# One tile pair's gate transposes on TensorE instead of by DMA, with re-planned engine orders, in a fused attention and MLP kernel

## The chip, the cores and the metric

One core of a Trainium2 chip. The metric is device time in microseconds (us) of one execution, lower is better. A profiled span is 1.7 to 1.9 us shorter than the time of the same execution in the runs of the kernel before, so spans are compared with spans and times with times. TensorE, VectorE, ScalarE, GpSimd and SyncE appear in the profile as PE (PEld for its weight loads), DVE, ACT, POOL and SP. The kernel before took 177.51 us (median of 3 runs, 177.42 to 177.81).

## The reference

Two branches work on one layer norm of x (2048 tokens, 448 columns, bf16) and are added up with x. Cut to what matters:

```python
xn = layernorm(x)
# A: linear attention, 16 heads of 28
q, k, v = split(xn @ wqkv)
phi_q = cat(softmax(q @ w_phi), softmax(-q @ w_phi))       # phi_k alike
o = (phi_q @ (phi_k.T @ v)) / (phi_q @ sum(phi_k) + 1e-6)
A = o @ wo
# B: token-shift mixer, then an MLP of 1792
h = gelu(layernorm(xn) @ w1)
hs = shift_tokens(h, (1, -1, 2, -2)) @ w2                  # four column groups, four shifts
x1 = xn + hs
B = x1 + gelu(layernorm(x1) @ w3) @ w4
return x + A + B
```

## The kernel before

The kernel is written for one core as a list of tasks. A planner places the tasks by a model (durations, PSUM slots, DMA delays) and by a table of ranks and earliest times; a recorder then emits each engine's instructions in that order and derives all semaphores. So most of a change of orders stands in a table of numbers, not in code. All instructions carry the line of a helper: L197 matmul, L201 transpose, L205 ScalarE, L209 VectorE and GpSimd, L212 DMA, L215 DMA transpose.

A second-layer tile pair (`W2`) gives the layer-normed gate tiles `g_tok`. They are transposed into `gT`, the right-hand side of the last stage's `H` matmuls (H = w3, then gelu; F = w4 and wo). In the kernel before every pair goes by a DMA transpose (`DMA_TRANSPOSE` in the profile), as do the transposes into `hT` that feed the second layer (indices shortened, cuts marked by dots):

```python
ga.append(P.add("ga%d" % i, dve, 320, ...))        # normalised gate tile into g_tok
def gd(t, j=j):
    R.dmaT(gT[:, slot, 2 * (j % 2):2 * (j % 2) + 2, :, :]..., g_tok[:, P.slot[("g", j)], :, :]...)
g_ready[i0] = g_ready[i1] = P.add("gD%d" % j, "SP", TI, G_RANK[j], ga, gd, gk, lag=TL2)
...
for d, i in enumerate((i0, i1)):                   # final addition and store, tile by tile
    def fin(t, ...):
        R.ew(dve, "tensor_tensor", outb[:, ob(i), u:v], bank(P.slot[k], d)[:, 0:v - u], xs[:, slot(i), u:v], op=ALU.add)
    def stor(t, ...):
        R.dma(outr[:, res_of(i), u:v], outb[:, ob(i), u:v], t.eng)
```

The softmax here doesn't subtract the row's maximum and nothing guards it: scores larger than these inputs give would overflow.

## Time and profile before

The prediction below shows the page, stretches, waits and chain of this kernel; they are not repeated. What matters of them:

| | kernel before |
|---|---|
| span, TensorE busy | 176.1 us, 169.2 us |
| waits of TensorE after the warm-up's start | wq 0.4, wv 0.5, hT 0.9, gT 0.3 us |
| H and F stage, 72.8 to 173.4 us | 0.11 us of idle |

TensorE is the bound, so the table is read from the waits: apart from the amount of TensorE's own work, only what ends one of them, or the start and the end around that work, can change the time.

The timeline of the kernel before from the last matmuls on (start, duration, engine, instruction, count, idle before):

```profile
172.91 1.45 SPq L212 DMA_DIRECT2D out_dram<-vaug  x2
173.31 0.69 DVE L209 TENSOR_TENSOR vaug<-ps,vaug 128x224 bf16<-128x224 f32 x2 [0.80 <-PE ps L197]
173.73 0.38 ACTq L212 DMA_DIRECT2D out_dram<-vaug  x1
```

Two additions of one half tile each, and a store behind each: the first goes out on the ACT queue at 173.73 while the second addition still runs. The SP entry at 172.91 merges two issues, one of them the last store, at 174.02.

### The profile page before, as it was taken

What the parts mean: (1) busy time and instruction counts of PE and PEld (TensorE: products, weight loads), DVE (VectorE), ACT (ScalarE), POOL (GpSimd) and SP (SyncE); (2) the same over time, 40 slices, a digit from 0 to 9 for tenths busy, and PEclk for the clock granted to TensorE, in tenths of its full rate; (3) what the DMA queues carried; (4) which work ended last, traced back from release to release, by engine and by line L of the source; (5) the groups of instructions that cost most, each with busy time, mean ns of one, the idle gap of its engine ahead of it and who ended that gap; (6) DMA issues with size and microseconds to landing.
All of it is one profiled execution on the core that took longest, in us unless ns stands there. A gap on an engine that the chain in (4) does not pass through costs nothing.

```text
span 176.1 us, 4846 instructions
## 1 busy us (share of the span) xinstructions
PE 169.2 (96%) x2080; PEld 111.4 (63%) x2080; DVE 116.4 (66%) x300; ACT 81.4 (46%) x116; POOL 77.8 (44%) x105
## 2 busy tenths in 40 slices
PE   5999999999999979999999999999999999999993
PEld 4766566676666665455555667655676666766793
DVE  3879999977995798995986655830654554370133
ACT  3398999999999510264557100327001561200000
POOL 7515578699339334035432253640037141261080
PEclk9999999999999999999999999999999999999999
DMA  6993444599918496625054616130010403313022
GB/s 146 279 339 83 72 83 91 101 360 327 331 49 162 77 122 123 119 32 93 0 98 86 120 27 149 53 63 0 0 56 26 89 0 63 60 52 63 0 86 78
DMA packets 41766, 18.30 MB, mean 104 GB/s; under 512 B 33552, under 2 KB 40848, under 8 KB 41744
## 3 DMA queue, kind: packets, MB, share of 16 engines
q1 hardware_dynamic: 41136, 17.91, 43.2%
q8 instruction: 16, 0.26, 0.6%
q10 hardware_dynamic: 608, 0.08, 0.3%
q14 instruction: 6, 0.05, 0.1%
HBM read 8.28 MB, written 1.84 MB: 57 GB/s over the span
## 4 chain that ended last, share of the span: by engine, by line
PE 86%; DMA 8%; SPq 3%; issue 1%; DVE 0%; DVEq 0%
PE ps L197 86%; DMA wv<-in_A_wqkv_dram 4%; SPq L212 3%; DMA hT<-hq 3%; DMA gT<-wv 2%; DVE vaug L209 0%; DVEq L169 0%; SPq L215 0%
## 5 line engine op out<-in xcount | busy, mean ns | idle before, releaser
L205 ACT ACTIVATE phik<-ps 128x1024 bf16<-128x1024 f32 (+1 forms) x44 | 41.3, 997 | 45.4 <-PE ps L197 45.4
L209 DVE TENSOR_TENSOR vaug<-ps,vaug 128x464 f32<-128x464 f32 (+3 forms) x66 | 32.8, 505 | 21.3 <-PE ps L197 15.9
L197 PE MATMUL ps<-w,phik 64*128 64x448 bf16 (+1 forms) x504 | 45.9, 328 | 0.0
L197 PE MATMUL ps<-gT,w 64*128 64x512 bf16 x392 | 44.5, 376 | 0.3 <-DMA gT<-wv 0.3
L197 PEld LDWEIGHTS ps<-w,phik 64*128 64x128 bf16 x504 | 29.5, 94 | 12.3 <-ACT phik L205 0.3
L197 PEld LDWEIGHTS ps<-gT,w 64*128 64x128 bf16 x392 | 23.0, 94 | 17.4 <-DVE vaug L209 0.7
L209 POOL TENSOR_TENSOR xnT<-vaug 128x224 bf16<-128x224 f32 x32 | 17.3, 564 | 27.7 <-DVE vaug L209 27.7
L209 POOL TENSOR_TENSOR vaug<-xn,xtok 128x448 f32<-128x448 bf16 x16 | 16.4, 1037 | 28.5 <-DVE vaug L209 26.4
L209 POOL TENSOR_TENSOR phik<-phik,ksum 128x896 bf16<-128x896 bf16 x14 | 24.1, 1749 | 8.2 <-DVE ksum L209 8.2
L209 POOL TENSOR_TENSOR rs<-rs,mhalf 128x2 f32<-128x2 f32 (+1 forms) x17 | 11.5, 683 | 28.3 <-DVE rs L209 22.0
L205 ACT ACTIVATE eq<-ps 120x1024 bf16<-120x1024 f32 (+1 forms) x18 | 17.5, 1045 | 6.1 <-PE ps L201 4.9
L209 DVE TENSOR_REDUCE ksum<-phik 128x32 f32<-128x896 bf16 x16 | 16.6, 1059 | 1.1 <-ACT phik L205 1.0
L209 DVE RECIPROCAL vaug<-ps 128x16 f32<-128x16 f32 x16 | 4.1, 254 | 19.1 <-PE ps L197 19.1
L197 PE MATMUL ps<-wo,xnT 64*128 64x448 bf16 (+1 forms) x126 | 14.1, 328 | 0.0
L197 PE MATMUL ps<-wv,xnT 64*128 64x448 bf16 x112 | 13.6, 349 | 0.5 <-DMA wv<-in_A_wqkv_dram 0.5
L197 PE MATMUL ps<-xnT,hq 64*120 64x512 bf16 x112 | 13.6, 377 | 0.0
L197 PE MATMUL ps<-wpk,xnT 64*128 64x448 bf16 x112 | 13.2, 349 | 0.0
L197 PE MATMUL ps<-w,hT 64*128 64x448 bf16 x56 | 12.1, 349 | 0.9 <-DMA hT<-hq 0.9
L197 PE MATMUL ps<-w2s,hT 64*128 64x448 bf16 x56 | 12.1, 350 | 0.0
L209 DVE BATCH_NORM_STATS2 st<-xtok 128x6 f32<-128x448 bf16 x16 | 9.2, 614 | 3.2 <-DMA xtok<-in_A_x_dram 3.2
L197 PE MATMUL ps<-w,xnT 64*128 64x448 bf16 x112 | 11.2, 349 | 0.0
L205 ACT ACTIVATE hq<-ps,fs 128x224 bf16<-128x224 f32 x32 | 11.0, 493 | 0.2
(71 smaller groups left out, 174.5 us busy)
## 6 DMA issues: line engine op xcount, KB each, us to landing
w<-in_B_w_dram SPq DMA_DIRECT2D x2, 896.0 KB, 7.0
w<-in_B_w_dram SPq DMA_DIRECT2D x1, 1568.0 KB, 12.3
out_dram<-vaug SPq DMA_DIRECT2D x14, 112.0 KB, 1.7
xtok<-in_A_x_dram SPq DMA_DIRECT2D x3, 448.0 KB, 7.0
eq<-in_A_wqkv_dram SPq DMA_DIRECT2D x2, 336.0 KB, 3.7
w<-in_B_w_dram SPq DMA_DIRECT2D x2, 336.0 KB, 7.3
wv<-in_A_wqkv_dram SPq DMA_DIRECT2D x1, 336.0 KB, 6.5
w2s<-in_B_w_dram SPq DMA_DIRECT2D x1, 336.0 KB, 5.4
```

Source lines behind the costliest of these rows:

```text
L197: self.op("PE", lambda e: e.matmul(out, lhsT, rhs, start=start, stop=stop, skip_group_check=True), [out], [lhsT, rhs], after=after)
L205: self.op("ACT", lambda e: e.activation(out, in_, func, **kw), [out], [in_] + aps)
L209: self.op(eng, lambda e: getattr(e, name)(out, *args, **kw), [out], aps)
L212: self.op(eng, lambda e: e.dma_start(out, in_), [out], [in_], dma=True)
```

## The change

Its intent is to take one of the DMA transposes out of the queue that TensorE waits for, and to plan all engine orders again with the delays of DMA transposes in the model. Four parts:

```diff
+        G_PE, G_ACT = (1,), ()
+            if j in G_PE:
+                def gtr(t, j=j, k2=k2):                       # gP1: eight TensorE transposes into PSUM
+                    for d in range(2):
+                        v = bank(P.slot[k2], d).bitcast(BF16)
+                        for c in range(4):
+                            R.tr(v[:, 128 * c:128 * c + 128], g_tok[:, slot, d, 128 * c:128 * c + 128], ident[:, :])
+                ...                                           # gPc2, gPc3: two copies PSUM -> gT (ACT or DVE)
+                continue                                      # no gD1
@@ planner's load model, and every rank and earliest time (two tables, left out)
-        RATE = {"x2": 5.4, "x4": 4.0, "x8": 2.6, "x12": 2.6}
+        RATE = {"x8": 3.0, "x12": 3.0, "w10": 3.0, "w11": 3.0, "w12": 3.0}
@@ zeros for the warm-up matmuls
+        z_spin = P.add("z_spin", dve, 350, -31, [], lambda t: R.ew(dve, "memset", kvq[:, 0:1, :, :], 0.0))
-            R.ew(dve, "memset", kvq[:, :, :, :], 0.0)
+            R.ew(dve, "memset", kvq[:, 1:2, :, :], 0.0)
@@ final additions and stores: one for a pair of tiles (18 stores become 9)
-                    for d, i in enumerate((i0, i1)):
-                            R.ew(dve, "tensor_tensor", outb[:, ob(i), u:v], bank(P.slot[k], d)[...], xs[...], op=ALU.add)
-                            R.dma(outr[:, res_of(i), u:v], outb[:, ob(i), u:v], t.eng)
+                        R.ew(dve, "tensor_tensor", rows(outb, "ob"), both(P.slot[k])[:, :, 0:v - u], rows(xs, "xs"), op=ALU.add)
+                        R.dma(outr[:, res_of(i0):res_of(i0) + 2, u:v], rows(outb, "ob"), t.eng)
```

The new orders in words: wv is loaded after w1; K0, K1, Q0, Q1 come before the first V; the two wrap-around matmuls (`nudge`) no longer stand together; TensorE runs one block of phik x vaug matmuls (`kv0`) before the fourth hT pair, where the kernel before runs two (`kv0`, `kv1`); one second-layer pair moves into the F stage.

## The prediction

> **What bounds the kernel now.** I read the busy times of the page first, then the table of stretches, the waits of TensorE, the chain that ended last, and the DMA issues.
>
> ```profile
> span 176.1 us, 4846 instructions
> PE 169.2 (96%) x2080; PEld 111.4 (63%) x2080; DVE 116.4 (66%) x300; ACT 81.4 (46%) x116; POOL 77.8 (44%) x105
> ```
>
> TensorE is busy for 169.2 of 176.1 us, so 6.9 us is all that any re-ordering could win. The stretches say where it lies (columns: busy time and instructions of each engine, then granted clock, DMA share, GB/s):
>
> ```profile
> 0.00:12.00 12.00, 9.69 (x110) 7.92 (x112) 7.17 (x29) 5.83 (x8) 6.39 (x23) 1.00 0.84 247
> 12.00:60.80 48.80, 48.23 (x491) 31.31 (x490) 42.87 (x92) 45.47 (x73) 32.35 (x26) 1.00 0.62 162
> 60.80:72.80 12.00, 10.76 (x208) 6.88 (x207) 11.23 (x25) 1.87 (x5) 3.41 (x4) 1.00 0.88 139
> 72.80:173.40 100.60, 100.49 (x1276) 65.32 (x1276) 54.49 (x156) 28.20 (x31) 35.62 (x52) 1.00 0.26 55
> 173.40:176.10 2.70, 0.00 (x0) 0.00 (x0) 0.60 (x2) 0.00 (x0) 0.00 (x0) 1.00 0.30 83
> ```
>
> The fourth stretch, 57% of the span, has 0.11 us of TensorE idle: nothing to win there, much to lose. The last 2.7 us are final additions, the last store's 1.6 us from issue to landing, and the end. What remains is named by the waits of TensorE (total, times, longest):
>
> ```profile
> PE ps L197 <- DVE kvq L209: 1.9, 1, 1.9
> PE ps L197 <- DMA hT<-hq: 0.9, 1, 0.9
> PE ps L197 <- DMA wv<-in_A_wqkv_dram: 0.5, 1, 0.5
> PE ps L201 <- DMA eq<-in_A_wqkv_dram: 0.4, 1, 0.4
> PE ps L197 <- DMA gT<-wv: 0.3, 1, 0.3
> ```
>
> [...]The other four sum to 2.1 us[...]. The chain shows both and what stood in front:
>
> ```profile
> 59.02 4.92 DMA hT<-hq
> 63.94 0.14 issue
> 64.08 5.09 PE ps L197 x92
> 69.17 0.05 SPq L215
> 69.22 0.04 issue
> 69.26 3.31 DMA gT<-wv
> 72.57 0.25 issue
> 72.82 100.50 PE ps L197 x1262
> ```
>
> At 63.94 the fourth transposed hidden tile pair lands, 4.92 us after its issue, and TensorE has waited for it. At 72.57 the gate tiles of pair 1 land; their issue had stood until 69.26 behind another transpose of the same queue, though the gate tiles were written by VectorE at about 66.9. This is the wait that the change aims at, and it costs 0.32 us.
>
> [...]
>
> ```profile
> 11.42 0.61 PE L201 MATMUL ps<-ident,xn 128*128 128x128 bf16 x8
> gT<-wv SPq DMA_TRANSPOSE x8, 3.3
> ```
>
> Eight on TensorE take 0.61 us in all, so they pipeline; a whole pair by DMA takes 3.3 us to land, its issue 1.24 us. [...]the 3.0 us minimum seen for these transposes [...]says that they must be issued early or hidden. [...]warm-up matmuls start every 0.20 us at first and every 0.10 us after about 6.4 us, 4.5 us from the first.
>
> **The change, part by part.**
>
> *Pair 1's transpose on TensorE.* Removes one of eight gT transposes from the queue (1.3 us of issue, 3.3 us of latency). Adds eight 128x128 transposes: 8 x 56 ns (spacing of the same instruction at 11.4 us) = 0.45 us of TensorE, which is the bound. They stand between two full-array kv groups, so they cost no extra change of array mode. Adds two evictions on ScalarE at about 0.5 us each (the same shape, xnT<-ps 128x512, took 0.59 us for one and 1.09 us for two); ScalarE is idle for 7.4 us in that stretch, so these are free. Gain: the 0.32 us wait. Net: +0.13 us.
>
> *The new orders.* In the compared orders, wv is loaded last of the early weights, and K0, K1, Q0, Q1 run before V0 and V1. So the 0.53 us wait for wv, which now lands at 13.29, goes: V starts some 4 x 1.4 = 5.6 us later. But ScalarE then has a fold eviction (0.86 us) and two xnT evictions (0.5 us each) to do before K1, and VectorE has tile 4's statistics (0.57 us) before the copy that tiles 2 and 3 need. From the durations of the trace I get K0 0.2 us later than its 11.96 us, and 0.25 us of waits at K1 and Q0. Net of the start: -0.1, plus 0.19 us of a stall at 29.1 that need not recur: -0.3 us.
>
> *The middle.* One V eviction moves from ScalarE to VectorE (2 instead of 3 there), worth 0.82 us, but the order of Q2, Q3 before K3 leaves ScalarE about 2 us without input near 25 us. So the 32 gelu evictions, now from 48.50 at 0.35 us each, begin at about 48.7. The fourth hT transpose then needs the 28th gelu and one wrapped block: 48.7 + 28 x 0.35 + 0.3 = 58.8, issue 59.0, against 59.02 now. With two more behind it in the queue it should land after 3.2 to 4.9 us, 62.2 to 63.9. TensorE reaches it at about 62.7 (first-layer matmuls to 56.7, three second-layer pairs 3 x 1.33, two nudges and one kv group 2.0). Wait left: about 0.6 of 0.93 us: -0.3 us. The nudges, now apart from kv, add two mode changes of about 0.08: +0.15 us.
>
> *Gate transposes by TensorE, in time.* VectorE finishes both gate tiles only after the addition of the fourth second-layer pair, at about 69.9; TensorE comes there at 70.3. No wait, but under half a microsecond of slack.
>
> *H stage.* The order puts the numerator groups and the first H blocks in other PSUM slots. The first numerator frees its slot after a queue of VectorE work, at about 82; a later H block wants that slot at about 81.2. I allow +0.3 us for this and its like, in a stretch that has no idle now.
>
> *Pairwise final addition and store.* One addition of 2x224 (about 0.6 us) for two of 0.38 us (0.69 us together), one store instead of two: the last landing 0.1 us earlier. Eighteen stores become nine; most were hidden.
>
> *Split memset.* Warm-up starts perhaps 0.6 us earlier[...]. 0.
>
> Sum: +0.13 - 0.3 - 0.3 + 0.15 + 0.3 - 0.1 = -0.1 us. The hand count sees only waits that I followed; a re-planned order[...] was probably made against just these waits and may remove more of the remaining 1.0 us than I found. I move my figure by -0.8 us for that, which is judgement and not working: about -0.9, that is 176.6 us.
>
> **Rivals.** (a) *All data waits go.* Take away 0.53 + 0.93 + 0.32 + 0.19 + part of the 0.4, add 0.6: -1.6 us, 175.9[...]. For it: a plan made for these very delays. Against: the hidden-tile wait hangs on ScalarE's gelu (93% busy in the second stretch), which the change hardly relieves. (b) *The wait only moves.* The first H block waits no more for gT by DMA but for ScalarE's copy, or the transposes wait for the gate tiles, since the fourth pair's addition now comes before them on VectorE (busy for 11.23 of 12 us there). Then 177.5 to 178.5. (c) *VectorE or PSUM slots become the bound in the H stage.* VectorE is 54% busy there on average, but single blocks have a few hundred ns of slack. One us of new stalls makes 178. (d) *DMA at the start:* x tiles before w1 and wv could bring statistics forward and the first K with them: up to -0.5 us.
>
> **Range and chances.** Two per cent is 3.55 us. To be faster by that, all four waits (2.1 us) would have to vanish, the added 0.6 us be free, and 1.5 us more come from the start or the end, where loads and the last store hold the time: 0.04. Slower by that needs 3.5 us of new stalls in orders that were planned with measured durations: 0.03. The range of 175.0 to 178.2 is (a) at its best to (b) and (c) together.
>
> **What would show it.** In the profile after: no wait on gT by DMA ahead of the first H block; eight ident,wv transposes of about 0.45 us between kv groups; no wait on wv; a wait on hT near 62 to 64 us, of 0 to 1 us; the first wpk matmul at 12.0 to 12.5; 100.5 us of H and F work (now with one second-layer pair in it) still nearly without idle; the last store 1.6 us from issue to landing. I am wrong if TensorE's idle after 12 us is above 3 us, or if the first K begins before 11.3 us, or if the hT wait is gone and the gelu ended before 58 us.

What no trace or run of this case shows, names of units among it, is cut out of it, and the cuts are marked. The sum: it came to -0.1 us, and -0.8 us of judgement made it about -0.9, that is 176.6 us. The 175 of rival (a) at its best, where the range begins, counted on a quicker start, and so did the reason why the split memset, put down as 0, might save time. "The other four" waits leave out the first, the 1.9 us before the warm-up matmuls; "both" are those for hT and gT.

Three of its statements are read from the matmul records of the kernel before. The transposes at 11.4 us start 56 ns apart and are recorded with 0.22 us each, so they overlap; those at 5.06 to 6.23 us still start 0.11 us apart. Pairs of 64-row matmuls start 0.19 us apart, and 0.28 us pass from such a pair to a 128-row matmul (60.59 to 60.87): 0.09 us for a change of array mode. In the changed kernel the eight transposes stand between 128-row matmuls, and starts there are 0.03 us (before the first) and 0.06 us (after the last) apart.

## The result, and the profile after

The changed kernel took 178.26 us (median of 6 runs, 178.05 to 178.52), the kernel before beside it 177.97 us (6 runs, 177.42 to 180.89, the slowest of them slow: over 1.5% above the fastest run of the same kernel; such runs here show a granted clock, the share of TensorE's full clock, of 0.981 wherever it is listed, as in b_kv2 and b_shift100). A ratio in this document is the mean time of one kernel's fast runs over that of the other's of the same rounds, so it is not quite the ratio of these medians: 1.0023, 95% interval 0.9999 to 1.0046. A second timing of the same kernel (a_same below) gave 1.0041 (1.0015 to 1.0068). So it is 0.2 to 0.4% slower (the first interval just includes no difference), within 2% as expected, but above the predicted range of 175.0 to 178.2, whose middle promised 0.9 us of gain.

The page of the changed kernel:

```profile
span 176.5 us, 4844 instructions
PE 169.4 (96%) x2088; PEld 105.2 (60%) x2088; DVE 113.3 (64%) x291; ACT 81.9 (46%) x118; POOL 79.6 (45%) x106
```

Eight more TensorE instructions (the transposes); on balance nine fewer on VectorE and two more on ScalarE. The same stretches as in the prediction, except that the last one runs to this kernel's end:

```profile
0.00:12.00 12.00, 9.42 (x110) 7.65 (x112) 7.79 (x32) 5.71 (x8) 6.38 (x23) 1.00 0.83 260
12.00:60.80 48.80, 48.74 (x493) 25.52 (x493) 40.81 (x93) 44.79 (x73) 34.19 (x27) 1.00 0.66 161
60.80:72.80 12.00, 10.77 (x201) 7.24 (x201) 10.63 (x24) 1.60 (x4) 4.11 (x5) 1.00 0.84 130
72.80:173.40 100.60, 100.48 (x1292) 64.81 (x1288) 53.49 (x146) 29.80 (x34) 34.88 (x51) 1.00 0.26 52
173.40:176.50 3.10, 0.00 (x0) 0.00 (x0) 0.54 (x1) 0.00 (x0) 0.00 (x0) 1.00 0.22 61
```

TensorE's idle grew from 2.31 to 2.58 us in the first stretch and fell from 0.57 to 0.06 in the second: the start gained 0.24 us, which the 0.2 us of added TensorE work takes. The third has the same 1.2 us of idle, the fourth is as full as before. The last is 0.4 us longer, and that is the difference of the two spans. The waits of TensorE:

```profile
PE ps L197 <- DVE kvq L209: 1.9, 1, 1.9
PE ps L197 <- DMA hT<-hq: 1.2, 1, 1.2
PE ps L201 <- DMA eq<-in_A_wqkv_dram: 0.7, 1, 0.7
```

Gone are the waits for wv and for gT. Grown is the wait for hT, from 0.9 to 1.2 us, and that for wq. The chain that ended last shows where hT stands and that the transposes took the place of gT:

```profile
58.22 4.79 DMA hT<-hq
63.01 0.14 issue
63.15 6.29 PE ps L197 x106
69.44 0.45 PE ps L201 x8
69.88 103.41 PE ps L197 x1318
173.32 0.62 DVE vaug L209
```

The fourth hT transpose is issued 0.8 us earlier than in the kernel before (58.22 against 59.02) and takes 4.79 us to land (4.92 there). TensorE is through with all that the order puts before it at 61.92, so it stands for 1.23 us. At 69.44 the eight transposes cost 0.45 us and wait for nothing.

The last matmul ends at about 173.3 in both kernels. What follows, in the timeline of the changed kernel:

```profile
173.32 0.62 DVE L209 TENSOR_TENSOR vaug<-ps,vaug 128x448 bf16<-128x448 f32 x1 [1.00 <-PE ps L197]
173.97 0.38 SPq L212 DMA_DIRECT2D out_dram<-vaug  x1
```

One addition of both half tiles, then one store of 112 KB. Read from the records of the trace (us):

```
                last matmul ends   last store: issue, landing, took   span ends   matmul to end
kernel before        173.30           174.02   175.61   1.59           176.11        2.81
changed kernel       173.28           173.97   175.78   1.81           176.53        3.25
```

The issue is 0.05 us earlier, but the larger store takes 0.22 us longer and lands 0.17 us later. Another 0.25 us come after the landing (0.75 us to the span's end instead of 0.50): in the changed kernel the last semaphore instruction of SP ends 0.3 us after those of the other engines, in the kernel before with them. The times show little of this last part: the two profiled executions took 178.05 and 177.84 us, 0.21 us apart, where their spans are 0.42 us apart.

### The profile page after: what moved, and what is told of

It is laid out like the page before. It is cut to its first block, busy times and chain, and to the rows that moved or that the text cites. A ratio compares the mean times of both kernels' runs of the same rounds, so it can differ in the third digit from the quotient of the medians.

```text
span 176.5 us, 4844 instructions
## 1 busy us (share of the span) xinstructions
PE 169.4 (96%) x2088; PEld 105.2 (60%) x2088; DVE 113.3 (64%) x291; ACT 81.9 (46%) x118; POOL 79.6 (45%) x106
## 4 chain that ended last, share of the span: by engine, by line
PE 91%; DMA 5%; SPq 2%; DVE 0%; issue 0%
PE ps L197 89%; DMA hT<-hq 3%; DMA eq<-in_A_wqkv_dram 2%; SPq L212 2%; PE ps L201 1%; DVE vaug L209 0%
## 5 line engine op out<-in xcount | busy, mean ns | idle before, releaser
L209 DVE TENSOR_TENSOR vaug<-ps,vaug 128x464 f32<-128x464 f32 (+3 forms) x57 | 31.8, 559 | 23.1 <-PE ps L197 17.4
L197 PE MATMUL ps<-gT,w 64*128 64x512 bf16 x392 | 45.1, 376 | 0.0
L197 PEld LDWEIGHTS ps<-gT,w 64*128 64x128 bf16 x392 | 21.5, 94 | 17.4 <-DVE vaug L209 0.2
L209 POOL TENSOR_TENSOR phik<-phik,ksum 128x896 bf16<-128x896 bf16 x15 | 25.8, 1757 | 4.3 <-DVE ksum L209 2.8
L197 PE MATMUL ps<-xnT,hq 64*120 64x512 bf16 x112 | 13.0, 377 | 0.0
L197 PE MATMUL ps<-wpk,xnT 64*128 64x448 bf16 x112 | 12.6, 349 | 0.1
L197 PE MATMUL ps<-wv,xnT 64*128 64x448 bf16 x112 | 12.3, 349 | 0.0
```

Source lines behind the costliest of these rows:

```text
L197: self.op("PE", lambda e: e.matmul(out, lhsT, rhs, start=start, stop=stop, skip_group_check=True), [out], [lhsT, rhs], after=after)
L209: self.op(eng, lambda e: getattr(e, name)(out, *args, **kw), [out], aps)
```

## The experiments

Fifteen variants ran, all correct. They also answer two questions of method. First, the landing of the wq load, on which the first folds wait, varies from 8.00 to 9.03 us between executions of kernels with the new load order and from 7.88 to 8.40 us in the four fast profiles with the old one, so two single profiles cannot be compared at their starts. I therefore take from each profile the time from that landing to the end of the last matmul ("wq to last matmul"). Second, that figure hardly scatters (165.42 and 165.50 us in two profiles with the order of before, 165.28, 165.18 and 165.09 in three with the new order), so it shows tenths of a microsecond where the times show only halves. (In the order of before, part of a late wq can hide behind the wait for wv, so its figure may also be a little lower.)

Runs share a chip and its runs of the kernel before: a_shift64, a_shift16, b_shift100 and a_tail one chip; a_same, a_kv1, a_gp_dma, b_gp, a_kv1_tail, a_wq, a_all and b_kv2 a second; b_pair, b_kv2_gp and a_kv12_tail a third. Medians are compared only within one chip.

Two theories of the hT wait were tested. **Fetch theory:** all over the trace a 16 KB packet appears on a DMA queue of kind "instruction", called a fetch here (16 of 16,384 bytes in each of the two kernels' profiles, 192 to 312 matmuls and weight loads apart, 250 on average, of 4,160 and 4,176), and takes 0.9 to 1.9 us; a DMA transpose on which one falls often lands 1 to 2 us late (the fourth hT of the changed kernel after 4.79 us, its first three after 3.05 to 3.21), and around it the packets of transposes nearly stop (in the changed kernel from some 200 in 0.25 us to 58, 10 and 44 from 62.0 us on, right after the fetch of 60.98 to 61.92). **Queue theory** (the prediction's): the transposes are late because three of them stand in the queue back to back.

The packet records of the changed kernel show what is late. All 1,024 data packets of the fourth hT had started before the fetch, and so had 30 of the 32 four-byte packets that close it; the last two came at 61.90 and 61.91, when the fetch ended. 15 of its 16 completions came at 61.27 to 61.43, the last at 63.01. The packets that stall from 62.0 on belong to the transpose behind it. Whether the fetch held one of the core's 16 DMA engines isn't shown: the records don't name a packet's engine. Where the fetch comes earlier, in a_shift16 below (60.06), the fourth hT's own data packets stall (from some 200 in 0.25 us to about 10, from 61.0 to 61.75).

### More TensorE instructions, to move the fetches: a_shift64, a_shift16, b_shift100

The columns of the warm-up matmuls are cut among more of them, which adds 64 (or 16, or 100) TensorE instructions before the first real work and changes nothing else:

```diff
-                R.mm(bank(P.slot[("ps", "spin")], 0)[:, 0:240], z[:, 0:128], z[:, 0:240], True, True)
+                m = 3 if n < 12 else 2
+                for j in range(m):
+                    R.mm(bank(P.slot[("ps", "spin")], 0)[:, 0:240 // m], z[:, 0:128], z[:, 0:240 // m], True, True)
```

> The changed kernel with 64 more TensorE instructions (32 more warm-up matmuls before the first real work; the columns of the warm-up are cut among them, so its length stays). Fetch theory: one of the 16 KB instruction-fetch packets moves from 60.98 us to about 58 us[...]; the 4th hT transpose (issued 58.22) then lands after about 3.1 us instead of 4.79, the wait of TensorE before the matmuls of that hT falls from 1.23 us of idle to under 0.3, and the time falls by 0.7 to 1.3 us, less up to 0.5 if another transpose (the one of hT 3, or xn tile 6, 7 or 15, over which a fetch would now fall) becomes late. Queue theory (the transposes land late because three of them stand back to back in the queue): landing 4.5 to 5 us, wait 1.1 to 1.3 us, time unchanged within 0.2 us.

Measured: 178.91 us, ratio 1.0071 (1.0050 to 1.0092), slower instead of faster. (In the changed kernel no DMA packet starts from 58.0 to 59.25 us, where the fetch was to go.) The waits:

```profile
PE ps L197 <- DVE kvq L209: 1.9, 1, 1.9
PE ps L197 <- DMA xnT<-xn: 1.0, 2, 0.8
PE ps L201 <- DMA eq<-in_A_wqkv_dram: 0.8, 1, 0.8
PE ps L197 <- DMA hT<-hq: 0.6, 1, 0.6
```

The hT wait halved, but a wait of 1.0 us for xn transposes is new. The fetches had moved, and the lateness with them: now the transposes of xn tiles 6, 7 and 15 (4.14, 3.56, 4.26 us instead of about 2.45) and of hT 3 (4.19 instead of 3.04) had a fetch on them, and those that had lost theirs (hT 7, gate pair 6) landed after 3.23 and 3.04 us instead of 3.91 and 4.71. Tile 15 is on the path. The fetch that I had wanted at 58 us came at 60.56, still on the fourth hT: it does not fall at an exact instruction (25 further on than in the changed kernel), and the late tile 15 had moved the rest. So the lateness went with the fetches again, and my forecast of the time failed.

> Control: the changed kernel with 16 more TensorE instructions (8 more warm-up matmuls). Fetch theory: the fetch moves only to about 60.2 us, still inside the packets of the 4th hT transpose, so its landing stays over 4 us and the time within 0.4 us of the changed kernel. Queue theory: no change either. What it tells apart from the run with 64 more is whether more and shorter warm-up matmuls by themselves change the time.

Measured: 177.78 us, ratio 1.0009 (0.9984 to 1.0034). Not the null result that I wrote: the fourth hT landed after 3.85 us, under the 4 us of the expectation, and its wait fell to

```profile
PE ps L197 <- DMA hT<-hq: 0.3, 1, 0.3
```

From wq to the last matmul it took 164.33 us, 0.85 less than a_same. No order was changed; three transposes still stand back to back. So queue position alone is not the cause; nor are the first three hT transposes of the changed kernel late (issued at 51.93, 53.62 and 54.97, landed after 3.06, 3.21 and 3.05 us), which stand as close to each other as the next three. And a hole in this place costs about what it seems to cost: 0.85 us for a wait that is 0.8 us shorter (0.3 against 1.1).

> The kernel before with 100 more TensorE instructions (50 more, shorter warm-up matmuls). Fetch theory: its fetch of 61.86 us moves to about 59, before the packets of the three hT transposes issued 59.02, 60.41, 61.71; their landings fall from 4.92, 4.36, 3.81 us to 3.1 to 3.4, and the wait of 0.93 us before the matmuls of hT at 64.08 goes nearly whole, time 0.5 to 1.0 us shorter. Queue theory: landings and time unchanged within 0.2 us.

Measured: 177.84 us, ratio 0.9983 (0.9947 to 1.0019), with two of six runs, the profiled one among them, slow. Its three hT transposes landed after 3.03, 3.26 and 3.45 us, as the fetch theory says, but the fetch of 59.86 us had hit the one before (4.55 us). The median counts the slow runs; the four fast ones took 176.78, 176.98, 177.14 and 178.53 us. Three of them have the expected gain, the fourth has not, and the interval of the ratio includes no difference, so the time doesn't tell the theories apart. Four profiles together, each with the same run of hT transposes (us, read from the records):

```
                    4th hT: issue   fetch starts   issue to landing   wait of TensorE
kernel before           59.02          61.86             4.92              0.93
changed kernel          58.22          60.98             4.79              1.23
  + 16 instructions     59.01          60.06             3.85              0.3
  + 64 instructions     59.68          60.56             4.13              0.6
```

Over 15 profiles (528 DMA transposes, with those of the later runs): call one hit when a fetch overlaps the stretch from 1.0 us after its issue to 0.25 us before its landing. After the first 40 us, 114 were hit, with a median of 4.10 us to landing, and 234 were not, with 3.10 (95% of them under 3.35, none over 3.62). A hit is not always late: 23 of the 114 landed within 3.35 us. The end of this stretch depends on the landing itself; with a fixed end of 2.85 us after the issue, 79 of 109 hit and 6 of 239 other transposes take over 3.62 us. Of the xn transposes before, 30 were hit (3.92 us) and 150 not (2.49).

### The ending alone: a_tail and b_pair

a_tail undoes the pairwise addition and store for the last half pair only:

```diff
+                        if u > 0:      # in fin: two additions;  in stor: two stores, on ACT and SP
+                            for d, i in enumerate((i0, i1)):
+                                R.ew(dve, "tensor_tensor", outb[:, P.slot[("ob", i)], u:v], bank(P.slot[k], d)[:, 0:v - u], ...)
```

> The changed kernel with only the last half pair of output tiles again added and stored tile by tile, as the kernel before has it: two additions of 224 columns, the first stored from the ACT queue, the second from SP. Tail theory: the store that ends last falls from 112 KB to 56 KB and lands after about 1.6 us instead of 1.81, and the time falls by 0.3 to 0.4 us. Rival (the 0.4 us at the end are only the scatter of the completion): within 0.15 us.

Measured: 178.31 us, ratio 1.0041 (1.0020 to 1.0062); no gain in time against the 1.0023 and 1.0041 of the changed kernel. In the trace the last store took 1.52 us and the matmul-to-end stretch is 2.97 us instead of 3.25; SP's last semaphore was still 0.3 us late. So a gain of 0.28 us, a little under the expected 0.3 to 0.4, is there in the profile; the times, with an interval of 0.4 us to either side, don't show it.

b_pair does the reverse: the kernel before with the last pair of tiles added and stored pairwise.

> The kernel before with only the last pair of output tiles added and stored as the changed kernel does it (two additions over both tiles, two stores of 112 KB on SP, none on ACT). Tail theory: from the last matmul to the end 3.0 us (the 0.2 of the larger store) to 3.25 us (with the late last SP semaphore) instead of 2.80; time 0.2 to 0.45 us above the kernel before, ratio 1.001 to 1.0025. Prediction on record for this part: 0.1 us faster. Rival: no difference in the ending, ratio 0.999 to 1.001.

Measured: 178.52 us, ratio 1.0034 (1.0011 to 1.0057): slower, against the step of 0.1 us faster. From the last matmul to the end it took 3.38 us instead of 2.81. This is more than either theory predicted: here the two last 112 KB stores are issued 0.8 us apart and took 2.30 and 2.20 us; in the changed kernel they are 1.6 us apart and take 1.8 (that the overlap is why was not tested). SP's last semaphore is not late here, so that part belongs to something else in the changed kernel; its cause is open.

### The changed kernel again, and the hole filled: a_same, a_kv1, a_kv1_tail, a_kv12_tail

> The changed kernel itself, as the measure for the other runs of this call: 177.8 to 178.4 us, ratio to the kernel before 1.000 to 1.005. Fetch theory: the transposes that are late (over 3.6 us from issue to landing, or over 3.0 for those of xn) are again those over whose packets an instruction fetch falls, and no others.

Measured: 178.46 us, ratio 1.0041 (1.0015 to 1.0068). Nine of its ten hit transposes were late, and no other was.

a_kv1 moves one task in TensorE's order after planning:

```diff
+        # kv1 goes to the place just ahead of W24.a, the first matmuls of the fourth hT
+        P.order.insert(index("W24.a"), P.order.pop(index("kv1")))
```

> The changed kernel with one swap in TensorE's order: the second block of 32 phik x vaug matmuls (1.08 us, its inputs long ready) goes ahead of the first matmuls of the 4th hT instead of behind them. If the 1.23 us of idle before that hT is really lost time that nothing gives back later, it fills with this work: wait under 0.3 us, time 0.8 to 1.1 us below that of the changed kernel. Rival (slack behind it absorbs the wait; the bound in this stage is the chain of VectorE normalisations and gate transposes that starts the last stage): a new wait before the gate transposes or the last stage, and a gain under 0.4 us.

Measured: 177.97 us, ratio 1.0009 (0.9986 to 1.0032), 0.5 us below a_same by the medians. The waits of TensorE:

```profile
PE ps L201 <- DMA eq<-in_A_wqkv_dram: 1.1, 1, 1.1
PE ps L197 <- DMA hT<-hq: 0.3, 1, 0.3
```

The hole shrank from 1.1 to 0.3 us, and wq to last matmul fell from 165.18 to 164.39 us: 0.79 us, at the foot of the expected 0.8 to 1.1; the 0.5 us in the times fall short of it, and in the profiled execution wq landed late (9.03 us), as the first line shows. So most of the hole was lost time.

a_kv1_tail adds stores per tile for all pairs and the last half pair as in a_tail:

> The changed kernel with the phik x vaug swap of the earlier run and with all stores again one per tile (18 stores; the last half pair also added tile by tile, its first store on the ACT queue). Seven profiles of the changed kernel's ending show 3.22 to 3.35 us from the last matmul to the end, three of the kernel before 2.80 to 2.81, the run with only the last half pair undone 2.97. Tail theory: 2.8 us again if the number of SP instructions sets the late last semaphore of SP, 2.97 if not; time 0.2 to 0.45 us below the swap alone, so 177.5 to 177.8 where the kernel before has 177.7, ratio 0.998 to 1.000. Rival (tail differences are hidden in other scatter): no difference from the swap alone, ratio 1.001.

Measured: 177.39 us, ratio 1.0006 (0.9969 to 1.0043; five runs at 177.26 to 177.98 and one at 179.21 with a granted clock of 0.990, which counts as fast). From the last matmul to the end it took 2.73 us (a_kv1: 3.22), and there is no late SP semaphore. By the medians it is 0.6 us below a_kv1. The ending is 0.49 us shorter in the profile; about 0.2 of that is the late semaphore, which the times hardly show.

> The changed kernel with stores per tile and two blocks of phik x vaug matmuls (2.16 us) ahead of the 4th hT instead of one. With one block ahead 0.3 us of wait for that hT is left; with two TensorE arrives after the landing, so the wait goes and nothing else of the order changes: 0.1 to 0.3 us below the run with one block and stores per tile, ratio 0.996 to 0.999. Rival (ACT or VectorE work that waits for those matmuls, or a later wait, takes it back): same as with one block.

Measured: 178.47 us, ratio 1.0041 (1.0025 to 1.0057), slower than with one block (ratio 1.0006; on two chips whose runs of the kernel before have the same median of 177.69 us, the medians are 1.1 us apart). The rival was right:

```profile
PE ps L197 <- DVE xn L209: 0.8, 2, 0.7
```

Two blocks ahead of the second-layer matmuls delay what VectorE makes of those, and the chain that ended last runs through VectorE's additions and statistics from 68 to 75.6 us. There is room for one block in the hole, not for two.

### The headline part: a_gp_dma and b_gp

a_gp_dma lets the DMA queue transpose gate pair 1 again, at the moment at which TensorE does it in the new order:

```diff
                 def gtr(t, j=j, k2=k2):
+                    R.dmaT(gT[:, slot, 2:4, :, :]..., g_tok[:, P.slot[("g", j)], :, :]...)
+                    return         # and the two copies emit nothing
```

> The changed kernel with its headline part undone in place: gate pair 1 again transposed by the DMA queue, at the moment where TensorE transposed it; no transposes on TensorE, no two copies; all else in the new order. The TensorE work falls by 0.45 us (eight transposes, 69.44 to 69.88). The gate tile would land about 3.1 us after an issue near 69.2, so at 72.3 or later, and its first matmul stood at about 71.8: a wait of 0.5 us or more, over 1.5 if a fetch falls on it. So 0 to 0.4 us slower than the changed kernel without a collision, about 1 us slower with one; if the transposes on TensorE were a loss, up to 0.4 us faster.

Measured: 182.61 us, ratio 1.0260 (1.0224 to 1.0295): 4.2 us slower, far more than expected. In the timeline the first H matmuls come at

```profile
74.00 1.04 PE L197 MATMUL ps<-gT,w 64*128 64x512 bf16 x8 [2.45 <-issue]
```

The queue was still busy with hT 7, which a fetch had slowed; the gate transpose went out at 70.65 and landed at 73.91. TensorE idles for 2.45 us, though eight transposes less were done. That profile was the quickest of the six runs (180.97 us, granted clock 0.999; 2.75 us above the profiled run of a_same). The other five have a clock of 0.987 to 0.990 and 182.06 to 182.97 us; why their clock is lower isn't shown.

b_gp is the other side: the kernel before with this part alone, in a PSUM slot that is free there (slot 0, after W26), all orders kept.

```diff
             def gd(t, j=j):
+                if j == 1:
+                    for d in range(2):
+                        for c in range(4):
+                            R.tr(bank(0, d).bitcast(BF16)[:, 128 * c:128 * c + 128], g_tok[:, slot, d, 128 * c:128 * c + 128], ident[:, :])
+                    ...                    # two ACT copies into gT
+                    return
```

> The kernel before with the headline part alone: its gate pair 1 transposed by eight TensorE transposes and copied by two ACT copies, at the place in the order where the DMA transpose was issued; every other order as before. The prediction's own sum for this part: 0.45 us of transposes and about 0.1 of changed shape against 0.32 us of wait with its 0.18 of refill that go, so +0.0 to +0.2 us on the kernel before. Rival (the path through the DMA queue is what holds the last stage back, and later gate and hT transposes move up too): 0.3 to 0.6 us faster.

Measured: 178.10 us, ratio 1.0017 (0.9994 to 1.0039). The expected +0.0 to +0.2 us lies in the interval (-0.1 to +0.7 us), the rival's -0.3 does not. (The 0.18 us of refill in the expectation is an estimate; in the kernel before, the first H matmul starts 0.67 us after the one ahead of it, where 0.19 is the pace: 0.48 us, of which 0.32 count as the wait and 0.16 do not.) Wq to last matmul 165.22 us against 165.42. By itself the part is worth about nothing; the new order, which uses the gate tiles earlier, cannot do without it.

### The start: a_wq and a_all

```diff
+        # the two wq loads go ahead of the load of x tiles 2 and 3 in SP's order
```

> The changed kernel with one change of its load order: the two wq loads before the 224 KB load of x tiles 2 and 3 instead of behind it. In seven profiles of the new load order wq lands at 8.00 to 9.03 us and TensorE waits 0.46 to 1.43 us for it, and from that landing to the last matmul it is 165.1 to 165.3 us whatever the landing. If that landing is what bounds the start: wq lands 0.5 to 0.8 us earlier, the wait falls to under 0.2, the time falls by 0.3 to 0.7 us. Rival: the x tiles 2 and 3 that now land later hold up VectorE's in-order work or the fold waits for its own copies; a wait of the same size before another matmul and a change under 0.2 us.

Measured: 178.74 us, ratio 1.0056 (1.0036 to 1.0077), no gain. Wq landed at 7.39 us and its wait is gone, but the rival was right: the load of x tiles 2 and 3, now behind it, landed at 7.99 us instead of 6.16 (changed kernel), VectorE's statistics follow it on the chain that ended last, and TensorE waits 0.3 us for VectorE's xn and 0.3 us for its copy of the folded weights. The first K came at 12.88 us, within the 11.98 to 13.01 of the new-order kernels with a later wq. So the landing of wq alone isn't the price of the start.

> All three on the changed kernel: wq loads earlier, swap, stores per tile. If the three add: 1.3 to 1.8 us below the changed kernel, about 176.7 to 177.0, ratio to the kernel before 0.993 to 0.996. If the start gives nothing: ratio 0.997 to 1.000.

Measured: 177.65 us, ratio 0.9998 (0.9976 to 1.0019): the second of the two forecasts, at its upper end.

### The same hole in the kernel before: b_kv2 and b_kv2_gp

> The kernel before with the same kind of swap: its third block of phik x vaug matmuls (1.08 us) ahead of the first matmuls of the hT that it waits 0.93 us for. If that wait is lost time there too: 0.6 to 0.9 us faster, ratio 0.995 to 0.997, and then the hole of the kernel before was never a reason for the re-planning to gain more than filling it by hand. If the next bound is close: under 0.3 us.

`kv2` moves ahead of `W26.a`. Measured: 177.19 us, ratio 0.9971 (0.9947 to 0.9995), faster by about 0.5 us.

> The kernel before with the swap of its phik x vaug block and the headline part (gate pair 1 transposed on TensorE) together. The swap alone gave 0.9971; in it TensorE then waits for a later hT or for the gate tile. If the transposes on TensorE (0.45 us of work) fall into such a wait and take the wait for the gate tile away: 0.2 to 0.5 us below the swap alone, ratio 0.994 to 0.996, the best of all so far. If they only add: ratio 0.998 to 1.000.

Measured: 177.30 us, ratio 0.9973 (0.9952 to 0.9995), the same as the swap alone, so no gain of the TensorE transposes is seen there. Its profiled span was 175.2 us, the shortest of all. What bounds it next:

```profile
PE ps L201 <- DMA eq<-in_A_wqkv_dram: 1.3, 1, 1.3
PE ps L197 <- DMA hT<-hq: 0.4, 1, 0.4
```

Both versions beat both kernels, by a swap of one task. The hT that it waits for now is a later one, hT 3, issued at 65.86 and landed after 4.33 us, with a fetch on it.

## Why the prediction was wrong

**Transposes on TensorE (+0.13): right.** 0.45 us for eight, no wait before them (the gate tiles were done at 68.8 us, not 69.9), the gT wait gone, copies hidden on ScalarE; b_gp measured the part alone at +0.17% with an interval that holds the +0.07% that 0.13 us are.

**Start (-0.3): right in kind.** The waits for wv and at 29.1 us went as said and K0 was not later (11.98 us), and in the one pair of profiles the gelu began at 48.10 us, not 48.7, and the fourth hT was issued 0.8 us earlier than before. The landing of wq moves the whole start by up to 1 us between executions, which I had not allowed for. The split memset did not start the warm-up earlier (1.89 us, before 1.88), which cost nothing, as I had put it down as 0.

**Middle, hT (-0.3): wrong, and with the wrong cause.** The landing (63.01) is in my 62.2 to 63.9, but TensorE arrived at 61.92 instead of 62.7. I had counted the one phik x vaug block of the new order; but the first-layer matmuls ended at 56.4 instead of 56.7, and that block and the two nudges, put down as 2.0 us, took 1.5 (1.08, 0.25 and 0.15 us from start to start). The wait grew by 0.3 us. The 0.15 us for mode changes isn't seen in the total either: TensorE's busy time grew by 0.24 us although the transposes added 0.45. I had put the lateness of these transposes down to their queue. Runs with shifted instruction streams and 528 transposes show that the late ones are mostly those that a fetch hits (over 3.62 us: 79 of 109 hit, 6 of 239 others), and that lateness moves with the fetches. A plan with one fixed delay for DMA transposes can't place the work around them: in the changed kernel those of hT take 3.0 to 4.8 us to land.

**H stage (+0.3): did not happen.** 0.12 us of idle against 0.11.

**Pairwise ending (-0.1): wrong sign.** +0.44 us in the profile (2.81 to 3.25), and b_pair and a_kv1_tail show the same direction in the times. I had counted two additions against one and assumed the store's 1.6 us for twice the bytes; it took 1.81. In the times the 0.44 is about 0.2 us by my estimate, since the two profiled executions are 0.21 us closer in time than in span.

**The -0.8 us of judgement: the step that failed the prediction.** Nothing in any run answers to it. The working's own sum was -0.1 us, that is 177.4. With the ending's error put right (0.54 us in the spans, an estimated 0.3 in the times) it would have been +0.2 to +0.4 us, 177.7 to 177.9, and the two timings say +0.4 and +0.7. Up to the last matmul my sum was about 0.0, and the profiles say -0.1 to -0.4 (165.1 to 165.3 against 165.4 to 165.5 us). That this came so near is partly luck: the hT wait was 0.6 us worse than my figure for it, while the H stage's 0.3 us and the 0.15 us of mode changes did not come. The allowance assumed that a plan made with the delays of DMA transposes had removed waits that I couldn't find. It had removed the waits for wv and gT that I had already counted, and made the largest one longer. Filling that hole and undoing the ending by hand (a_kv1_tail) is worth about 1.1 us on the changed kernel by the medians, and then it equals the kernel before; the hole was as easy to fill in that one (b_kv2).

**Left open:** the late last SP semaphore (0.3 us) of the changed kernel; why a transpose lands about 1 us after the fetch on it has ended (63.01 against 61.92 us), and why the packets of the next one stall then; what takes back part of b_kv2's and a_all's gains beyond the waits named.

## What to carry to other kernels

Do not add to a worked sum a gain that no view of the profile supports; an order from a planner is only as good as its model, and its holes can be counted in the compared orders (here: how many ready blocks stand before a late transpose). Look at what the final store is before pairing operations: bytes on the last transfer are on the path even if all other stores are hidden (1.81 us for 112 KB, 1.59 for 56 KB). Where a DMA transpose lands late, look for a packet on the instruction queue before blaming the queue (here a median of 4.10 us with one on it, 3.10 without), and keep a block of ready matmuls in front of its consumer.
